# First attention of a four-layer kernel: two more lots of eight projection units with paired 64-row remainders

## The chip, the cores and the metric

The kernel runs on one core of a Trainium2 chip. The metric is the device time of one execution in microseconds, the median of several runs. The engines are named as in the profile: PE (TensorE matmuls), PEld (its weight loads), DVE (VectorE), ACT (ScalarE), POOL (GpSimd) and SP (SyncE, which here issues DMAs only).

## The reference

Four layers with residuals are applied to x of 2048 tokens by 576, in bf16: attention A, mixer B, A, B, and each takes the layer norm of x. Only the attention matters here:

```python
H = 32; Dh = 18; W, dil = 8, 2
q, k, v = split(layernorm(x) @ wqkv)          # 576 -> 3 * 576
logits = q . k[pos - 2 * w], w in 0..7        # * Dh ** -0.5, masked ahead of the start
x = x + (softmax(logits) . v) @ wo
```

The mixer B (4608 wide, with a 2048 x 2048 token matrix) takes most of the time and is not touched.

## The kernel before

The tokens are kept transposed in `xnT` as 128 rows by 5 chunks by 2048 tokens. 576 features are 4 chunks of 128 rows and a remainder of 64 rows, chunk 4. Rows 64 to 127 of chunk 4 come from the last 64 columns of the normalized row (`ln_xn` columns 576 to 639), which are zero in the first attention, and the remainder's weights `wqk4` have zeros in rows 64 to 127, so that chunk 4 is multiplied over whole rows too.

**Projection units.** `PG(d, qk, cc)` computes 128 columns (block d of 5) of q or k (qk) for 512 tokens (cc of 4): five matmuls of 128x512 (L462) into one PSUM bank, a cast of the bank into a staging tile (`evac`, L443 on DVE or L445 on ACT), and, when both halves of 1024 tokens and q and k of a block are staged, DMAs of the staged rows into `QK` ("QK moves"), dealt in turn to the queues of SP and POOL. Block d=4 holds the rest of q and k together. Staging tiles are `stgs` or `lent` parts of `win2a`. A staging tile is written again only when the moves out of it have landed. `PG_run`, which before uses only in the second attention, takes eight units at once in eight banks (three of `X0`, five of the ring): chunks 0 to 3 of the first four, then the eight 64-row remainders alternating between the upper and the lower half of the rows, then chunks 0 to 3 of the other four. For this, the lower half must hold the data and the weights a second time.

**The attention's loop.** The tokens are 17 query tiles, each in two halves of 16 heads: 34 steps s. `L_mm(s)` computes the logits (L536, 16 matmuls; heads are spread over 8 groups g, step 2t needs g 0 to 3 and step 2t+1 g 4 to 7) into a tile of three banks, X, of which there is one, and one of Y. `EXP(s)` is ACT's exponential of the X part and then of the Y part (L545). `PV(s)` multiplies by v (L559) into a ring bank, and DVE normalizes. A step issues L_mm(s+1), EXP(s+1), PV(s) and then what the table `at(s, ...)` lists: projections, `VW(t, hh)` (v of half a tile, L451, cast to `v_ext`), `O_T` (transposes, L595), `WO` (output projection, L629). Because X exists once, L_mm(s+1) waits for the X part of EXP(s). `QK` also has constant rows for the masks, which `fill_window_rows(QK, half)` copies for 1024 tokens from `win_pat` (L201 and L204, DVE).

**The order around the change** is written out by hand for PE, ACT, DVE, POOL and SP; each engine executes its instructions in that order. In the first attention the start is: load x and weights; statistics (`S_`), power for the inverse deviation (`R_`, its power on POOL, L728), normalization (`A_`, L735) and transposes (`T_pe` on PE for tiles 0 to 3, `T_` as DMA transposes issued by SP for the others) for tiles of 128 tokens; `VW` of tiles 0 to 3; `load_pat` on SP; the fill of the first half; 18 units of cc 0 and 1 one after the other, with `R_(12, 4)` behind the units of d=2 of cc 1; eight `VW` (tiles 4 to 7); `A_` and `T_` of tiles 12 to 15; then the list `pre`: four units of cc 2, L_mm(0) and EXP(0), a fifth unit, the fill of the second half, three more units; the two `VW` of tile 8; then the loop. Steps 0 to 9 have one unit each; from step 10 on every step that is not a multiple of four has a `VW`.

Of the kernel before, what the change touches and what calls it, by code (L numbers as in the profile page):

```python
# [18 lines left out]
P = 128  # L19
D = 576  # L20
# [43 lines left out]
class K:  # L64
# [316 lines left out]
    def layer_A(self, li):  # L381
        nc, tc, cfg = self.nc, self.tc, self.cfg
# [9 lines left out]
        QK = main.tile([P, 2, 8, XW], bf16, name="QK")  # L392
# [10 lines left out]
        RING, NSLOT = 6, 2  # L403
        oT = main.tile([P, 5, RING * P], bf16, name="oT")
# [10 lines left out]
        wqk, wqk4, wv_sb, wo_sb = R["wqk"], R["wqk4"], R["wv"], R["wo"]  # L415
# [31 lines left out]
        def VW(t, hh, dve):  # L447
            nk = tdim(t)[0]
            pv = self.PT_tile([P, 512], f32, "pv")
            for c in range(5):  # L450
                nc.tensor.matmul(pv[:nk, 0:288], lhsT=self.xnT[:, c, k0_(t):k0_(t) + nk],  # L451
                                 rhs=wv_sb[:, c, hh * 288:(hh + 1) * 288], start=(c == 0), stop=(c == 4))
            evac(v_ext[:nk, t, 16 * hh:16 * hh + 16, 0:DH], pv[:nk, 0:288].rearrange("p (b d) -> p b d", d=DH), dve)
# [4 lines left out]
        def PG_mm(pp, d, qk, cc, c, start, stop, half=None):  # L458
            w0 = d * P + (640 if qk else 0)
            r0, r1 = (0, P) if half is None else (64 * half, 64 * half + 64)  # L460
            w = wqk[:, c, w0:w0 + P] if c < 4 else wqk4[r0:r1, w0:w0 + P]
            nc.tensor.matmul(pp, lhsT=w, rhs=self.xnT[r0:r1, c, cc * 512:(cc + 1) * 512],  # L462
                             start=start, stop=stop, tile_position=(r0, 0))

        def PG_run(units, queues, on_dve, between=None):
            banks = ([X0[:, k_, :] for k_ in range(3)] +
                     [self.PT_tile([P, 512], f32, "pp")[:, :] for k_ in range(len(units) - 3)])
            n = len(units) // 2
            for u in range(n):
                for c in range(4):  # L470
                    PG_mm(banks[u], *units[u], c, c == 0, False)
            for u in range(2 * n):
                PG_mm(banks[u], *units[u], 4, u >= n, u < n, half=u % 2)
            for u in range(2 * n):
                if u >= n:
                    for c in range(4):
                        PG_mm(banks[u], *units[u], c, False, c == 3)
                if u == n and between:
                    between()
                PG(*units[u], u in on_dve, queues(units[u][0]), pp=banks[u])  # L480

        def PG(d, qk, cc, dve, queues=(nc.sync, nc.gpsimd), pp=None):

            cb, gi = divmod(cc, CBW // 512)
            alone = bool(lent) and d == 4 and cb == 1
            key = (d, cc if alone else cb, alone)
            if key not in stg_tiles:
                if alone:
                    stg_tiles[key] = lent[1]
                elif cb == 0 and d >= 3 and lent:  # L490
                    stg_tiles[key] = lent[d - 3]
                else:
                    stg_tiles[key] = stgs[d if li == 0 else stg_rr[0] % NSTG]
                    stg_rr[0] += 1
                stg_left[key] = 1 if alone else (2 if d < 4 else 1) * (CBW // 512)
            stg = stg_tiles[key]
            if pp is None:
                pp = self.PT_tile([P, 512], f32, "pp")[:, :]
                for c in range(5):
                    PG_mm(pp, d, qk, cc, c, c == 0, c == 4)  # L500
            evac(stg[:, qk, gi * 512:(gi + 1) * 512], pp, dve)
            stg_left[key] -= 1
            if stg_left[key] == 0:
                stg_tiles.pop(key)
                cs = slice(cc * 512, (cc + 1) * 512) if alone else slice(cb * CBW, (cb + 1) * CBW)
                ss = slice(gi * 512, (gi + 1) * 512) if alone else slice(0, CBW)
                moves = []
                for h in range(d * P // DH, H):
                    a, b = max(h * DH, d * P), min((h + 1) * DH, (d + 1) * P)
                    if a >= b:  # L510
                        break
                    g, rg = divmod(h, 4)
                    q0, s0, n = 32 * rg + a - h * DH, a - d * P, b - a
                    if d < 4:
                        moves.append((QK[q0:q0 + n, :, g, cs], stg[s0:s0 + n, :, :]))
                    else:
                        for a_ in range(2):
                            moves.append((QK[q0:q0 + n, a_, g, cs], stg[64 * a_ + s0:64 * a_ + s0 + n, 0, ss]))
                for dst, src in moves:
                    dma_rr[0] += 1  # L520
                    self.dma(dst, src, eng=queues[dma_rr[0] % len(queues)])

        NST = 2 * NT
# [149 lines left out]
        q2 = (nc.gpsimd, nc.sync, nc.gpsimd)  # L673


        if li == 0:
            xts = {}
            spare = oT[:].rearrange("p a b -> p (a b)")[:, 0:4 * D].rearrange("p (i d) -> p i d", d=D)

            def x_load(xg, i0, n, eng):  # L680
                self.dma(xg, self.rows_of(self.A_x, i0, n).rearrange("(i p) d -> p i d", p=P), eng=eng)
# [38 lines left out]
            def S_(*tiles):  # L720
                for i in tiles:
                    B_(i)
                    G_(i)

            def R_(i0, n):
                rs = rstds[:, i0:i0 + n]
                nc.vector.tensor_scalar_add(out=rs, in0=mvs[:, i0:i0 + n, 1], scalar1=EPS)
                nc.gpsimd.tensor_tensor(out=rs, in0=rs, in1=self.neg_half[:, 0:1].to_broadcast([P, n]), op=ALU.pow)  # L728
            xns = {}

            def A_(*tiles):
                for i in tiles:
                    xns[i] = xn = self.xn_bufs[self.xn_rr % len(self.xn_bufs)]
                    self.xn_rr += 1
                    nc.vector.tensor_scalar(out=xn[:, 0:D], in0=xts[i], scalar1=mvs[:, i, 0:1],  # L735
                                            scalar2=rstds[:, i:i + 1], op0=ALU.subtract, op1=ALU.mult)

            def T_pe(i):
                xn = xns.pop(i)
# [7 lines left out]
            def T_(*tiles):  # L747
                for i in tiles:
                    self.ln_T(xns.pop(i), i * P, P)
# [26 lines left out]
            rows[3](nc.gpsimd)  # L776
            A_(6, 7)
            T_(6, 7)
            S_(8)
            self.load_pat(nc.sync)  # L780
            S_(9, 10, 11)
# [3 lines left out]
            T_(8, 9, 10, 11)  # L785
            self.fill_window_rows(QK, 0)
            S_(13, 14, 15)
            order = [(d, cc) for cc in range(2) for d in range(5)]
            for k_, (d, cc) in enumerate(order):
                for qk in ((1, 0) if d < 4 else (0,)):  # L790
                    PG(d, qk, cc, False, (nc.gpsimd, nc.sync) if d in (0, 3, 4) else q2)
                if k_ == 7:
                    R_(12, 4)
            nvw0, nvw = 4, 9
        else:
            def qs(d):
                return (nc.gpsimd, nc.sync) if d == 0 else q2
# [11 lines left out]
            for cc in range(2):  # L809
                PG(4, 0, cc, False, q2)  # L810
            nvw0, nvw = 0, 4
        for t in range(nvw0, nvw - (1 if li == 0 else 0)):
            for hh in range(2):
                VW(t, hh, li == 0 and hh == 0)
        if li == 0:
# [13 lines left out]
        def at(s, f, *a):  # L829
            table.setdefault(s, []).append((f, a))  # L830
        pgs = [(d, qk, cc) for d, cc in ((0, 2), (1, 2), (2, 2), (0, 3), (1, 3), (2, 3), (3, 2), (3, 3), (4, 2), (4, 3))
               for qk in ((1, 0) if d < 4 else (0,))]
        PG_END = 14
        pre, pgs = pgs[:6], pgs[6:]
        if li == 0:
            for u in ((3, 1, 2), (3, 0, 2)):
                pre.append(u)
                pgs.remove(u)
        if li == 0:
            pgs = [u for u in pgs if u[2] == 2] + [u for u in pgs if u[2] > 2]  # L840
        for k_, (d, qk, cc) in enumerate(pgs):
            at(k_ if li == 0 else (k_ * PG_END) // len(pgs), PG, d, qk, cc, True, *((q2,) if li == 0 else ()))
        vws = [(t, hh) for t in range(nvw, NT) for hh in range(2)]
        lag, twice = (PG_END - 5, (PG_END - 2, NST - 2)) if li == 0 else (9, (NST - 2,))
        vsteps = ([x for x in range(PG_END - 4, NST - 3) if x % 4] if li == 0 else
                  [6, 6] + list(range(8, NST)))
        for k_, (t, hh) in enumerate(vws):
            assert vsteps[k_] <= 2 * t - 2 + hh
# [58 lines left out]
            at(s_b + d_b * k_, win2b_piece, k_)  # L907
        at(NST - 2, O_T, NT - 2)
        at(NST, O_T, NT - 1)
        for k_, (d, qk, cc) in enumerate(pre):  # L910
            if k_ == (4 if li == 0 else 0):
                self.ring = ["PT"]
                L_mm(0)
                EXP(0)
            PG(d, qk, cc, li > 0 or k_ < 5, q2)
            if li == 0 and k_ == 4:
                self.fill_window_rows(QK, 1)
        if li == 0:
            VW(nvw - 1, 0, False)
            VW(nvw - 1, 1, False)  # L920
        for s in range(NST):
            if s == NST - 1:
                self.ring = ["PT", "PT", "PT", "Y", "Y"]
# [345 lines left out]
```

## Time and profile before

| | |
|---|---|
| time, median of 3 runs | 1152.67 us (1152.64 to 1152.9) |
| time of the profiled execution | 1152.74 us |
| its span | 1150.9 us |
| granted TensorE clock | 1.00 |
| first projection unit of the first attention | 13.42 us |
| first logits, second, third | 42.16, 48.14, 50.14 us |

All stage times below are microseconds from the span's start. In the views an instruction group has its start and length, the engine, the line, the tiles as out<-in, the shape, the count, and in brackets the idle time in front of it with what ended it. The rows of PE's matmuls overlap: one of 128x512 lasts 0.38 us by its row, and the next starts 0.216 us after it.

### The profile page before, as it was taken

What the parts mean: (1) busy time and instruction counts of PE and PEld (TensorE: products, weight loads), DVE (VectorE), ACT (ScalarE), POOL (GpSimd) and SP (SyncE); (2) the same over time, 40 slices, a digit from 0 to 9 for tenths busy, and PEclk for the clock granted to TensorE, in tenths of its full rate; (3) what the DMA queues carried; (4) which work ended last, traced back from release to release, by engine and by line L of the source; (5) the groups of instructions that cost most, each with busy time, mean ns of one, the idle gap of its engine ahead of it and who ended that gap; (6) DMA issues with size and microseconds to landing.
All of it is one profiled execution on the core that took longest, in us unless ns stands there. A gap on an engine that the chain in (4) does not pass through costs nothing.

```text
span 1150.9 us, 29693 instructions
## 1 busy us (share of the span) xinstructions
PE 1142.6 (99%) x12930; PEld 614.5 (53%) x12949; DVE 539.7 (47%) x1198; ACT 370.5 (32%) x660; POOL 259.6 (23%) x387
## 2 busy tenths in 40 slices
PE   8999999999999999999999999999999999999998
PEld 5567554444444444457755775544444444444676
DVE  8789987312233222244466889843322223222312
ACT  5589565011111111102247876541111111011000
POOL 3689654000000000002153767530000000000000
PEclk9999999999999999999999999999999999999999
DMA  8877696000000000049455867920000000001322
GB/s 195 183 164 200 141 211 137 10 13 13 13 1 13 13 13 2 1 152 213 110 110 110 180 152 176 246 60 1 13 13 13 13 13 1 13 2 30 101 74 58
DMA packets 177372, 91.26 MB, mean 79 GB/s; under 512 B 128788, under 2 KB 170420, under 8 KB 177242
## 3 DMA queue, kind: packets, MB, share of 16 engines
q1 hardware_dynamic: 164762, 70.75, 28.1%
q0 software_dynamic: 5888, 12.72, 4.6%
q10 hardware_dynamic: 6592, 5.90, 1.7%
q8 instruction: 101, 1.65, 0.6%
q14 instruction: 29, 0.24, 0.1%
HBM read 35.46 MB, written 14.69 MB: 44 GB/s over the span
## 4 chain that ended last, share of the span: by engine, by line
PE 97%; ACT 1%; DVE 1%; issue 0%; DVEq 0%; ACTq 0%
PE hh L234 79%; PE pp L462 6%; PE pv L451 3%; PE pw L629 3%; PE O_ps L559 3%; PE L_ps L536 2%; ACT P_sb L545 1%; PE L_ps L462 1%; PE hh L1191 0%; PE pt L595 0%; DVE ln_st L715 0%; DVE ln_xn L735 0%; DVE win_bits L158 0%; ACT v_ext L445 0%; ACT xnT L745 0%
## 5 line engine op out<-in xcount | busy, mean ns | idle before, releaser
L234 PE MATMUL hh<-Wq,Z 64*128 64x512 bf16 x4608 | 505.8, 376 | 0.0
L234 PEld LDWEIGHTS <-Z 64*128 64x128 bf16 x6984 | 339.8, 94 | 310.1
L1095 DVE TENSOR_TENSOR g_tmp<-hh,ln_xn 128x512 f32<-128x512 f32 x144 | 92.8, 686 | 452.3 <-PE hh L234 452.3
L947 ACT COPY bank_turn<-ones 1x1 bf16<-1x1 bf16 x239 | 44.8, 188 | 538.5 <-PE hh L234 538.5
L78 POOL DMA_DIRECT2D wout<-in_B_w_out_dram x4 | 4.3, 1075 | 602.0 <-PE hh L234 602.0
L234 PE MATMUL hh<-wout,Z 64*128 64x288 bf16 x2232 | 137.0, 283 | 0.0
L545 ACT ACTIVATE P_sb<-L_ps 128x1440 bf16<-128x1440 f32 (+3 forms) x136 | 125.0, 971 | 24.6 <-PE L_ps L536 23.2
L234 PE MATMUL hh<-xnT,w 64*128 64x512 bf16 x1152 | 132.2, 376 | 0.0
L234 PE MATMUL hh<-win2a,xnT 64*128 64x512 bf16 (+1 forms) x960 | 118.7, 355 | 0.0
L234 PEld LDWEIGHTS <-xnT 64*128 64x128 bf16 x1440 | 69.9, 94 | 70.0 <-issue 0.5
L1020 DVE BATCH_NORM_STATS2 z_st<-zp 128x6 f32<-128x512 bf16 (+1 forms) x160 | 93.0, 624 | 13.0 <-ACT zp L1018 12.9
L1086 ACT ACTIVATE z1T<-hh 128x1024 bf16<-128x1024 f32 x72 | 73.7, 1024 | 61.9 <-PE hh L234 61.9
L234 PEld LDWEIGHTS <-w 64*128 64x128 bf16 x1152 | 56.1, 94 | 68.3
L1096 DVE TENSOR_TENSOR Z<-g_tmp,z1T 128x512 bf16<-128x512 f32 x144 | 92.4, 683 | 0.0
L1018 ACT ACTIVATE zp<-hh 128x1024 bf16<-128x1024 f32 (+1 forms) x96 | 76.1, 810 | 48.8 <-PE hh L234 48.6
L462 PE MATMUL pp<-xnT,wqk_sb 128*128 128x512 bf16 (+1 forms) x313 | 74.2, 379 | 0.9
L234 PE MATMUL hh<-win2b,xnT 64*128 64x512 bf16 (+1 forms) x480 | 72.8, 355 | 0.0
L1160 DVE TENSOR_TENSOR x_new<-hh,xo 128x288 bf16<-128x288 f32 x64 | 26.3, 453 | 93.0 <-PE hh L234 85.0
L299 POOL TENSOR_SCALAR ln_xn<-x_new,ln_mv,ln_rstd 128x576 bf16<-128x576 bf16 x28 | 64.2, 2293 | 2.7
L78 POOL DMA_DIRECT2D QK<-stg x76 | 48.0, 636 | 36.5 <-DVE stg L443 21.9
L462 PEld LDWEIGHTS <-wqk_sb 128*128 128x128 bf16 (+1 forms) x360 | 32.1, 97 | 36.6 <-issue 1.9
L1044 POOL TENSOR_SCALAR Z<-zp,z_mv,z_rstd 128x256 bf16<-128x256 bf16 x32 | 50.7, 1584 | 3.5
(124 smaller groups left out, 753.3 us busy)
## 6 DMA issues: line engine op xcount, KB each, us to landing
xres<-x_new SPq DMA_DIRECT2D x44, 144.0 KB
wout<-in_B_w_out_dram POOLq DMA_DIRECT2D x4, 1296.0 KB, 7.4
xo<-xres SPq DMA_DIRECT2D x32, 144.0 KB
xn_rows<-ln_xn SPq DMA_DIRECT2D x28, 160.0 KB
w<-in_B_w_in_dram SPq DMA_DIRECT2D x16, 256.0 KB
QK<-stg POOLq DMA_DIRECT2D x51, 72.0 KB, 4.4
QK<-stg SPq DMA_DIRECT2D x37, 72.0 KB
xo<-in_A_x_dram SPq DMA_DIRECT2D x6, 288.0 KB
```

What stands on the lines that cost most here:

```text
L78: return eng.dma_start(out=out, in_=in_)
L234: ins = self.nc.tensor.matmul(outs[a_], lhsT=lhs(a_, c, r0), rhs=rhs(a_, c, r0), start=start and k_ == 0, stop=stop and k_ == len(chunks) ...
L299: e.tensor_scalar(out=xn[:nrows, 0:D], in0=x_t[:nrows, :], scalar1=mv[:nrows, 0:1], scalar2=rstd[:nrows, 0:1], op0=ALU.subtract, op1=ALU.mult)
L462: nc.tensor.matmul(pp, lhsT=w, rhs=self.xnT[r0:r1, c, cc * 512:(cc + 1) * 512], start=start, stop=stop, tile_position=(r0, 0))
L545: nc.scalar.activation(out=P_bufs[2 * jp + s % 2][:nk, :, :, 0:nq], in_=Lv[:nk, :, :, 0:nq], func=ACT.Exp, scale=scale)
L947: self.turn_on = lambda tok: nc.scalar.copy(out=tok, in_=self.ones[0:1, 0:1])
L1018: nc.scalar.activation(out=zp[:, w0:w0 + n], in_=pz, func=ACT.Gelu_apprx_tanh)
L1020: nc.vector.bn_stats(out=st[:, x // 512, :], in_=zp[:, x:x + min(512, w0 + n - x)])
L1044: eng.tensor_scalar(out=Z[:, b0:b1, i, :], in0=zv[:, b0:b1, :], scalar1=mv[:, 0:1], scalar2=rstd[:, 0:1], op0=ALU.subtract, op1=ALU.mult)
L1086: lambda ht, z1T=z1T, q2=q2: nc.scalar.activation(out=z1T[:, q2 * 512:(q2 + 2) * 512], in_=ht[:].rearrange("p a b -> p (a b)"), func=ACT.G ...
L1095: nc.vector.tensor_tensor(out=tmp[:], in0=pg[:, a_, :], in1=bsp[:, qs], op=ALU.add)
L1096: nc.vector.tensor_tensor(out=uT(jj)[:, sub, qs], in0=tmp[:], in1=z1Ts[jj, sub][:, qs], op=ALU.mult)
```

## The change

Eight of the nine units of cc 1 and the eight first units of cc 2 become two calls of `PG_run`. For this the last 64 columns of the normalized rows are copied a second time for tiles 4 to 11 (eight copies on DVE), and the 64 remainder rows of the weights are loaded a second time into rows 64 to 127 of the end of `oT` (two DMAs on SP, ahead of `load_pat`). The second lot is ahead of L_mm(0); the fill of the second half is issued in the middle of this lot, behind its first four casts, of which DVE makes the second and the fourth and ACT the others, as it does the lot's last four. `R_(12, 4)` is issued in the middle of the first lot, behind the moves of d=0 and d=1, where it was behind those of d=2. The unit (4, 0, 2) goes from step 0 to `pre`, its cast from DVE to ACT. The two `VW` of tile 9 go from steps 10 and 11 to step 0, and the later ones are dealt anew, so that steps 10 and 14 have none.

```diff
         def PG_mm(pp, d, qk, cc, c, start, stop, half=None):
...
-            w = wqk[:, c, w0:w0 + P] if c < 4 else wqk4[r0:r1, w0:w0 + P]
+            w4 = wqk4_up if li == 0 and half == 1 else wqk4
+            w = wqk[:, c, w0:w0 + P] if c < 4 else w4[r0:r1, w0:w0 + P]
...
-            spare = oT[:].rearrange("p a b -> p (a b)")[:, 0:4 * D].rearrange("p (i d) -> p i d", d=D)
+            oT_flat = oT[:].rearrange("p a b -> p (a b)")
+            spare = oT_flat[:, 0:4 * D].rearrange("p (i d) -> p i d", d=D)
+            wqk4_up = oT_flat[:, RING * P * 5 - 2 * D:RING * P * 5]
+
+            def load_wqk4_up(eng):
+                for c0, w0 in ((D, D + 64), (0, 0)):
+                    self.dma(wqk4_up[64:128, w0:w0 + 512], self.A_wqkv[512:576, c0:c0 + 512], eng=eng)
...
                     nc.vector.tensor_scalar(out=xn[:, 0:D], in0=xts[i], scalar1=mvs[:, i, 0:1],
                                             scalar2=rstds[:, i:i + 1], op0=ALU.subtract, op1=ALU.mult)
+                    if 4 <= i < 12:
+                        nc.vector.tensor_copy(out=xn[:, D:640], in_=xn[:, 512:D])
...
             T_(6, 7)
+            load_wqk4_up(nc.sync)
             S_(8)
             self.load_pat(nc.sync)
...
-            order = [(d, cc) for cc in range(2) for d in range(5)]
-            for k_, (d, cc) in enumerate(order):
+            for d in range(5):
                 for qk in ((1, 0) if d < 4 else (0,)):
-                    PG(d, qk, cc, False, (nc.gpsimd, nc.sync) if d in (0, 3, 4) else q2)
-                if k_ == 7:
-                    R_(12, 4)
-            nvw0, nvw = 4, 9
+                    PG(d, qk, 0, False, (nc.gpsimd, nc.sync) if d in (0, 3, 4) else q2)
+            PG_run([(d, qk, 1) for d in range(4) for qk in (1, 0)],
+                   lambda d: (nc.gpsimd, nc.sync) if d in (0, 3) else q2, (), lambda: R_(12, 4))
+            PG(4, 0, 1, False, (nc.gpsimd, nc.sync))
+            nvw0, nvw = 4, 10
...
-        for t in range(nvw0, nvw - (1 if li == 0 else 0)):
+        for t in range(nvw0, 8 if li == 0 else nvw):
...
-            for u in ((3, 1, 2), (3, 0, 2)):
+            for u in ((3, 1, 2), (3, 0, 2), (4, 0, 2)):
...
-            at(k_ if li == 0 else (k_ * PG_END) // len(pgs), PG, d, qk, cc, True, *((q2,) if li == 0 else ()))
+            at(k_ + 1 if li == 0 else (k_ * PG_END) // len(pgs), PG, d, qk, cc, True, *((q2,) if li == 0 else ()))
...
-        vsteps = ([x for x in range(PG_END - 4, NST - 3) if x % 4] if li == 0 else
+        vsteps = ([x for x in range(PG_END - 3, NST - 3) if x % 4 and x != PG_END] if li == 0 else
...
+        if li == 0:
+            PG_run(pre[:8], lambda d: q2, (1, 3), lambda: self.fill_window_rows(QK, 1))
+            pre = pre[8:]
         for k_, (d, qk, cc) in enumerate(pre):
-            if k_ == (4 if li == 0 else 0):
+            if k_ == 0:
                 self.ring = ["PT"]
                 L_mm(0)
                 EXP(0)
-            PG(d, qk, cc, li > 0 or k_ < 5, q2)
-            if li == 0 and k_ == 4:
-                self.fill_window_rows(QK, 1)
+            PG(d, qk, cc, li > 0, q2)
         if li == 0:
-            VW(nvw - 1, 0, False)
-            VW(nvw - 1, 1, False)
+            VW(8, 0, False)
+            VW(8, 1, False)
+            at(0, VW, 9, 0, True)
+            at(0, VW, 9, 1, False)
```

## The prediction

> **What bounds the kernel now.** The page first:
>
> ```profile
> PE 1142.6 (99%) x12930; PEld 614.5 (53%) x12949; DVE 539.7 (47%) x1198; ACT 370.5 (32%) x660; POOL 259.6 (23%) x387
> ...
> PE 97%; ACT 1%; DVE 1%; issue 0%; DVEq 0%; ACTq 0%
> ```
>
> PE is busy for 99% of the span and is 97% of the chain that ended last. So whatever PE is spared comes off the time, and whatever PE is made to wait goes onto it. The change lies between 13 and 82 us, so next come PE's instructions in order of time there (start, length, line, tiles, count).
>
> ```profile
> 13.42 19.59 PE L462 MATMUL pp<-xnT,wqk_sb 128*128 128x512 bf16 x88
> 32.84 5.06 PE L451 MATMUL pv<-wv_sb,xnT 128*128 128x288 bf16 x40
> 37.74 4.48 PE L462 MATMUL pp<-xnT,wqk_sb 128*128 128x512 bf16 x19
> 42.16 0.40 PE L536 MATMUL L_ps<-QK 32*128 32x128 bf16 x16
> ...
> 48.14 0.40 PE L536 MATMUL L_ps<-QK 32*128 32x128 bf16 x16
> ...
> 50.14 0.39 PE L536 MATMUL L_ps<-QK 32*128 32x120 bf16 x16 [0.23 <-ACT P_sb L545]
> ```
>
> The 18 units of the first 1024 tokens are 90 matmuls (two records are missing) in 32.84 - 13.42 = 19.42 us: 0.216 us a matmul, 1.08 us a unit, without a pause. Eight VW follow in 37.74 - 32.84 = 4.90 us. The first logits, L_mm(0), come at 42.16, L_mm(1) at 48.14, L_mm(2) at 50.14 after a wait of 0.23 us. Before has next to nothing to win in waits here, and much to lose.
>
> **The pairs.** In a lot, eight 64-row remainders run two at a time: 36 slots for 40. Before runs the same routine in its second attention:
>
> ```profile
> 580.65 2.76 PE L462 MATMUL L_ps<-xnT,wqk_sb 128*128 128x512 bf16 x11
> ...
> 584.22 0.60 PE L462 MATMUL L_ps<-xnT,wqk_sb 64*128 64x512 bf16 x3
> ...
> 588.65 1.03 PE L462 MATMUL L_ps<-xnT,wqk_sb 128*128 128x512 bf16 x4
> ...
> 584.86 1.56 ACT L445 CAST stg<-L_ps 128x512 bf16<-128x512 f32 x3 [1.94 <-PE pp L462]
> ```
>
> The first and third row are the starts of its first and second lot: 8.00 us for one. (The others, its first remainder and its first cast, are used below.) 40 slots are 8.64 us, so a lot saves 0.64 us and two save 1.28 us. Pure pairing would be 36 x 0.216 = 7.78 us a lot; 0.22 us more is paid for going from whole rows to half rows and back. The Trainium skill, "TensorEngine Tiling (Array Packing)", Tiling Modes, states that changing the tiling mode drains TensorE; the trace agrees with 0.22 us for two changes. By its "up to 2x" for 64 rows the two lots would save 1.73 us instead.
>
> **The copies on DVE.** A_ gets eight copies of 128x64, each waiting for the operation in front of it. The nearest row is the fill's own:
>
> ```profile
> 24.71 2.36 DVE L201 COPY QK<-win_pat 128x4096 bf16<-128x4096 bf16 x2 [0.39 <-DMA win_pat<-win_period]
> 27.11 0.18 DVE L204 COPY QK<-win_pat 128x64 bf16<-128x64 bf16 x1
> 27.20 2.35 DVE L201 COPY QK<-win_pat 128x4096 bf16<-128x4096 bf16 x2
> ...
> 44.45 4.62 DVE L201 COPY QK<-win_pat 128x4096 bf16<-128x4096 bf16 x4
> ```
>
> From 24.71 + 2.36 = 27.07 to 27.20 is 0.13 us. Two big copies take 2.36 us and four 4.62 us, so neighbours that don't wait for each other overlap by 0.10 us, which is lost too. One copy costs about 0.20 us (bounds 0.13 and 0.25), eight 1.6 us. The fill of the first half then starts later by 1.6 less the 0.39 us for which it waited anyway: 1.2 us. The transposes of tiles 4 to 7 land about 0.5 us later, which I put at nothing: cc=1 starts at 23.1, and their issue ends at 20.2 before.
>
> **SP.** The two loads of load_wqk4_up come between these transposes and load_pat:
>
> ```profile
> 4.59 4.50 SPq L78 DMA_DIRECT2D wqk_sb<-in_A_wqkv_dram  x6
> ...
> 14.03 6.20 SPq L306 DMA_TRANSPOSE xnT<-ln_xn  x4
> 21.81 1.60 SPq L78 DMA_DIRECT2D win_pat<-win_period  x4
> ```
>
> At 4.50 / 6 = 0.75 us each they fill the gap from 20.23 to 21.81; load_pat starts some 0.4 us later, which the late fill covers (if not, the fill waits as it does now). Their data are wanted at 26.7, when the first lot reaches its remainders. SP's own QK moves then begin about 0.8 us later, behind tiles 8 to 11.
>
> **POOL's queue of QK moves** decides the rest. POOL issues 23 moves for the first 1024 tokens:
>
> ```profile
> 28.02 6.28 POOL L78 DMA_DIRECT2D QK<-stg  x9 [5.19 <-DVE QK L204]
> ...
> 37.78 1.04 POOL L728 TENSOR_TENSOR lnx_rstd<-lnx_rstd,neg_half 128x4 f32<-128x4 f32 x1
> 38.77 4.84 POOL L78 DMA_DIRECT2D QK<-win2a  x8
> ```
>
> It is released by the fill and then never pauses to 43.61: nine moves, six more (d=2), R_(12,4)'s power, eight of d=3 and d=4. In the change the start is 1.2 us later and the power goes ahead of the six, so that d=2 comes 2.2 us later and d=4, the last four, from 41.2 + 1.2 = 42.4 on. Before, the fill of the second half began at 44.45, behind the last issue. In the change it stands right behind the two casts that DVE has in the second lot. PE is there at 23.13 + 8.00 + 1.08 + 4.90 = 37.1, the first banks are done 4.2 us later (584.86 - 580.65 there), and the casts take 1.3 us: the fill runs from about 42.5 to 47.1, on top of d=4. What that does, the second attention shows:
>
> ```profile
> 597.44 4.62 DVE L201 COPY QK<-win_pat 128x4096 bf16<-128x4096 bf16 x4
> ...
> 596.55 5.62 POOL L78 DMA_DIRECT2D QK<-stg  x5
> ...
> 602.17 2.90 POOL L78 DMA_DIRECT2D QK<-stg  x5
> ...
> 597.59 4.87 SPq L78 DMA_DIRECT2D QK<-stg  x6
> ```
>
> Five moves on POOL take 5.62 us while DVE copies and 2.90 us after it: about one passes for each copy of 1.15 us. SP's take 0.81 us all the same. The Trainium skill, "DMA: Bandwidth & Descriptors", SWDGE vs HWDGE vs iDMA, states that GpSimd writes its descriptors to SBUF, that DVE locks it out of there during 2-port modes, and that DMAs from SP are immune; by that rule the change is in trouble here, and the trace agrees (5.62 against 2.90 us). So the last issue runs from about 46.2 to 47.3 instead of 44.3 to 44.8. From issue to landing:
>
> ```profile
> QK<-win2a POOLq DMA_DIRECT2D x1, 36.0 KB, 4.6
> ...
> DMA to landing us min/median/max: 4.3/4.3/4.3
> ...
> DMA to landing us min/median/max: 3.5/4.9/7.5
> ```
>
> 4.6 us is the last move before (43.1 to 47.7, just 0.4 us ahead of L_mm(1)), 4.3 us one under the second attention's copies, and the third row is all QK moves from 26 to 52 us. I take 4.7, between the like case's 4.3 and the 5.2 that the last move of before becomes with 0.6 us more of issue: d=4 has landed at 50.9 (bounds by the third row, 49.7 and 53.7).
>
> **Who waits for d=4.** The last four matmuls of L_mm(1), which need the last heads, and the cast of (4,0,2), which overwrites lent[1], from which d=4 is moved. Before, that cast was DVE's and came at step 0; now it is ACT's and stands ahead of two v_ext casts and EXP(1).
>
> ```profile
> 42.69 1.94 ACT L545 ACTIVATE P_sb<-L_ps 128x1536 bf16<-128x1536 f32 x2 [4.34 <-PE L_ps L536]
> 44.91 0.59 ACT L445 CAST stg<-pp 128x512 bf16<-128x512 f32 x1 [0.28 <-ACT P_sb L545]
> ...
> 48.24 0.40 ACT L445 CAST v_ext<-pv 128x288 bf16<-128x288 f32 x1 [0.21 <-PE pv L451]
> 48.64 3.82 ACT L545 ACTIVATE P_sb<-L_ps 128x1536 bf16<-128x1536 f32 x4
> ```
>
> From 50.9, 0.59 + 0.40 + 0.40 us, a little overlapped (1.3), puts EXP(1) at 52.2 against 48.64, and L_mm(2), which waits for its X part, 3.6 us later too: 53.7. PE cannot use the time: PV(0) needs the bank of (4,0,2), the two moved VW are done by 53.5, and PE's own work would have reached L_mm(2) at 50.14 - 1.28 + 1.26 = 50.1. EXP(0) is late too, but not on the path: d=2's last move, issued 0.58 us ahead of the power's 37.78 before, is issued near 39.4 and, at the median 4.9 us, landed at 44.3; four casts (2.2 us) and EXP(0) (1.94 us) end at 48.5, two microseconds ahead of 50.9. The loop after L_mm(2) is the same in both, and PE-bound to step 9, so the lateness is kept.
>
> **What comes back.** Steps 10 and 14 lose a VW each. From the chain in order of time:
>
> ```profile
> 69.24 0.32 PE L_ps L536 x16
> ...
> 71.68 0.32 PE L_ps L536 x16
> ...
> 78.24 0.32 PE L_ps L536 x16
> ...
> 80.30 0.32 PE L_ps L536 x16
> ...
> 82.35 0.38 PE L_ps L536 x16
> ...
> 84.20 0.39 PE L_ps L536 x16
> ```
>
> A step with little PE work is 1.85 us (82.35 to 84.20: logits, their exponentials, the next logits), so step 14 can fall from 2.06 to 1.85 and step 10 from 2.44 to about 1.95: 0.7 us (bounds 0.2, if ACT is behind, and 1.26, all of both VW).
>
> **The sum.** +3.6 - 0.7 = +2.9 us; the 1.28 us of the pairs are inside the 3.6, since PE waits anyway. The profiled execution took 1152.74 us (span 1150.9), 0.07 us over the median of 1152.67. So 1152.7 + 2.9 = **1155.6 us**.
>
> **Rivals.**
> - *The fill and d=4 miss each other* (the copies cost less, or the casts hold the fill back). Then d=4 lands at 47.7 + 1.2 = 48.9, EXP(1) starts at 50.2, L_mm(2) is 1.6 us late, less 0.7: +0.9, 1153.6 us. Against it: one move of shift either way still leaves three under the copies. For it: all of this is a matter of 0.6 us per move. Chance 0.18.
> - *The moves are in time, and the gain stays* (the eight copies vanish in DVE's waits). This decides if d=4 has landed by about 47.9. Then EXP(0) runs at 45.8 behind the last cast of the lot, EXP(1) at 48.5, L_mm(2) at 50.0, and steps 10 and 14 give 0.7: -0.8, 1151.9 us. To be faster by over 2.3 us all of the 1.28 and 1.26 us would have to come off at once. For it: the pairs are sure. Against it: the fill has only 0.39 us of slack and the moves 0.4 us. Chance 0.12.
> - *The last moves get caught in what SP issues next* (tiles 12 to 15, then xo and wo_sb). With 7.0 us instead of 4.7, d=4 lands at 53.2: +5.2, 1157.9 us. The 7.5 us in the row above was such a case. Chance 0.08.
> - That the pairs would not overlap is excluded by the 8.00 us lot.
>
> **The numbers.** The forecast has 0.62. Its own range, from 49.7 us and 52.4 us for d=4's landing, is 1154.4 to 1157.1. With the first rival inside and the other two left out, the range is 1152.4 to 1157.6. A change under 0.2% (2.3 us) is about what a measurement of this kernel can tell from none. Slower by more, over 1155.0: most of the forecast, 0.48 (d=4 landed after 50.3), and the third rival, 0.08: 0.56. Within: the rest of the forecast, the first rival and most of the second: 0.41. Faster: 0.03.
>
> **What would show it.** Right: lots of 8.0 us at 23 and 37 us; the fill of the first half at about 25.9; four POOL moves of over 1 us near 43 to 47; EXP(1) near 52.2 and L_mm(2) near 53.7, with the ACT cast of (4,0,2) released by a DMA; the same steps as before to step 9. Wrong: POOL done before the second fill, or EXP(1) before 50.

## The result, and the profile after

| | before | after |
|---|---|---|
| time, median of 6 runs | 1152.79 us (1152.53 to 1153.44) | 1157.48 us (1156.79 to 1158.61) |
| ratio | | 1.0036 (95%: 1.0026 to 1.0046) |
| profiled execution, its span | 1152.74, 1150.9 us | 1158.61, 1156.8 us |
| L_mm(0), L_mm(1), L_mm(2) | 42.16, 48.14, 50.14 | 45.16, 50.19, 56.09 |
| first matmul of the mixer (L234) | 121.40 | 126.67 |

The change makes the kernel slower by 4.7 us by the medians, 0.4%. The profiled execution of after is the longest of its six runs, so what it shows is the upper end, and those of e3, e4 and e11 below are among the shortest of theirs. From L_mm(2) on it is 5.95 us late, from the mixer on 5.27 us.

The page of after, its busy times and its chain:

```profile
PE 1144.9 (99%) x12949; PEld 615.8 (53%) x12949; DVE 538.4 (47%) x1202; ACT 371.6 (32%) x664; POOL 261.9 (23%) x387
...
PE 95%; ACT 1%; POOL 1%; DMA 1%; DVE 1%; issue 1%; DVEq 0%; ACTq 0%
```

POOL and DMA have come into the chain, which before had 97% PE and neither of them. Where, PE in order of time says:

```profile
23.12 2.75 PE L463 MATMUL L_ps<-xnT,wqk_sb 128*128 128x512 bf16 x12
...
37.09 2.75 PE L463 MATMUL L_ps<-xnT,wqk_sb 128*128 128x512 bf16 x12
...
45.16 0.40 PE L537 MATMUL L_ps<-QK 32*128 32x128 bf16 x16
47.36 1.24 PE L463 MATMUL pp<-xnT,wqk_sb 128*128 128x512 bf16 x5 [1.80 <-ACT stg L445]
...
50.19 0.60 PE L537 MATMUL L_ps<-QK 32*128 32x128 bf16 x14 [0.36 <-ACT P_sb L546]
51.56 0.22 PE L537 MATMUL L_ps<-QK 32*128 32x128 bf16 x1 [0.78 <-DMA QK<-win2a]
52.20 0.23 PE L537 MATMUL L_ps<-QK 32*128 32x128 bf16 x1 [0.41 <-DMA QK<-win2a]
53.17 0.58 PE L560 MATMUL O_ps<-v_ext,P_sb 128*128 128x19 bf16 x16 [0.75 <-ACT win2a L445]
53.60 2.56 PE L451 MATMUL pv<-wv_sb,xnT 128*128 128x288 bf16 x10
56.09 0.45 PE L537 MATMUL L_ps<-QK 32*128 32x120 bf16 x16
```

The lots run at 23.12 and 37.09. The last matmuls of L_mm(1) wait for moves out of `win2a`, which is d=4, until 52.20, PV(0) for the cast of (4,0,2) until 53.17, and then the two VW of tile 9 take 2.56 us instead of the 1.39 us of the same ten matmuls at tile 8. POOL's queue in the same time:

```profile
29.32 6.25 POOL L78 DMA_DIRECT2D QK<-stg  x9 [5.65 <-ACT stg L445]
35.59 1.03 POOL L735 TENSOR_TENSOR lnx_rstd<-lnx_rstd,neg_half 128x4 f32<-128x4 f32 x1
36.58 3.74 POOL L78 DMA_DIRECT2D QK<-stg  x6
40.32 1.84 POOL L78 DMA_DIRECT2D QK<-win2a  x3
42.98 5.38 POOL L78 DMA_DIRECT2D QK<-win2a  x5 [0.82 <-DMA QK<-stg]
```

It starts at 29.32, waits 0.82 us for the landing of an earlier move, and needs 5.38 us for the last five moves. DVE has the two fills, and ACT goes on when d=2 and d=4 have landed:

```profile
25.99 2.36 DVE L201 COPY QK<-win_pat 128x4096 bf16<-128x4096 bf16 x2
28.39 0.18 DVE L204 COPY QK<-win_pat 128x64 bf16<-128x64 bf16 x1
...
43.14 4.62 DVE L201 COPY QK<-win_pat 128x4096 bf16<-128x4096 bf16 x4
```

```profile
27.31 1.56 ACT L445 CAST stg<-L_ps 128x512 bf16<-128x512 f32 x3 [3.40 <-PE pp L463]
...
46.73 1.07 ACT L445 CAST stg<-pp 128x512 bf16<-128x512 f32 x2 [3.48 <-DMA QK<-stg]
...
48.64 1.99 ACT L546 ACTIVATE P_sb<-L_ps 128x1536 bf16<-128x1536 f32 x2
52.53 0.58 ACT L445 CAST win2a<-pp 128x512 bf16<-128x512 f32 x1 [1.91 <-PE L_ps L537]
53.02 0.71 ACT L445 CAST v_ext<-pv 128x288 bf16<-128x288 f32 x2
53.60 1.97 ACT L546 ACTIVATE P_sb<-L_ps 128x1536 bf16<-128x1536 f32 x2
```

POOL's row names a cast as what released the first move, but it is the fill that held it. The first move begins 28.39 + 0.18 = 28.57 to 29.32, 0.75 us, behind the fill's first small copy (L204), as before the change, where it was 27.29 to 28.02, 0.73 us. In all profiles but those of e2 and e4 it begins 3.31 to 3.35 us after the fill does. The lot's first casts alone would have let it go at about 28.7, as e4 shows below. The casts at 46.73, ahead of EXP(0), wait for d=2. The chain that ended last, in order of time, goes from the landing of a move out of `stg` (37.17 to 42.70) over POOL's last moves, the landing of the last one (47.86 to 52.15), the last matmul of L_mm(1), the cast of (4,0,2), PV(0) and the two VW of tile 9 to L_mm(2).

Last, the windows (start:end, length, busy time and instructions of PE, PEld, DVE, ACT and POOL, then the granted clock, the DMA share and GB/s):

```profile
50.70:53.20 2.50, 0.56 (x5) 0.31 (x5) 0.00 (x0) 0.67 (x2) 0.00 (x0) 0.93 1.18 277
53.20:56.10 2.90, 2.90 (x30) 1.72 (x29) 1.17 (x3) 2.37 (x4) 2.69 (x6) 0.50 1.11 354
56.10:60.00 3.90, 3.90 (x78) 2.33 (x78) 2.12 (x5) 3.68 (x5) 0.91 (x2) 0.98 0.38 102
```

PE was busy for 0.56 of the 2.50 us in the first row. In finer windows the granted clock falls to 0.50 at 52.85 and is back at 1.00 at 56.26.

### The profile page after: what moved, and what is told of

Same layout as the page of the kernel before. It is cut to its first block, busy times and chain, and to the rows that moved or that the text cites. A ratio compares the mean times of both kernels' runs of the same rounds, so it can differ in the third digit from the quotient of the medians.

```text
span 1156.8 us, 29718 instructions
## 1 busy us (share of the span) xinstructions
PE 1144.9 (99%) x12949; PEld 615.8 (53%) x12949; DVE 538.4 (47%) x1202; ACT 371.6 (32%) x664; POOL 261.9 (23%) x387
## 4 chain that ended last, share of the span: by engine, by line
PE 95%; ACT 1%; POOL 1%; DMA 1%; DVE 1%; issue 1%; DVEq 0%; ACTq 0%
PE hh L234 79%; PE pp L463 4%; PE pv L451 3%; PE pw L630 3%; PE O_ps L560 2%; PE L_ps L537 2%; ACT P_sb L546 1%; POOL QK L78 1%; PE L_ps L463 1%; DMA QK<-stg 0%; PE hh L1204 0%; DMA QK<-win2a 0%; DVE ln_st L722 0%; PE pt L596 0%; ACT stg L445 0%
## 5 line engine op out<-in xcount | busy, mean ns | idle before, releaser
L234 PE MATMUL hh<-Wq,Z 64*128 64x512 bf16 x4608 | 505.8, 376 | 0.0
L234 PEld LDWEIGHTS <-Z 64*128 64x128 bf16 x6984 | 340.3, 94 | 309.6
L234 PE MATMUL hh<-wout,Z 64*128 64x288 bf16 x2232 | 137.0, 283 | 0.0
L234 PE MATMUL hh<-xnT,w 64*128 64x512 bf16 x1152 | 132.2, 376 | 0.0
L234 PE MATMUL hh<-win2a,xnT 64*128 64x512 bf16 (+1 forms) x960 | 118.7, 355 | 0.0
L234 PEld LDWEIGHTS <-xnT 64*128 64x128 bf16 x1440 | 70.0, 94 | 69.9 <-issue 0.5
L234 PEld LDWEIGHTS <-w 64*128 64x128 bf16 x1152 | 56.1, 94 | 68.2
L234 PE MATMUL hh<-win2b,xnT 64*128 64x512 bf16 (+1 forms) x480 | 72.8, 355 | 0.0
L463 PE MATMUL pp<-xnT,wqk_sb 128*128 128x512 bf16 (+1 forms) x294 | 68.2, 379 | 1.8 <-ACT stg L445 1.8
L1057 POOL TENSOR_SCALAR Z<-zp,z_mv,z_rstd 128x256 bf16<-128x256 bf16 x32 | 50.8, 1588 | 3.5
```

Source lines behind the costliest of these rows:

```text
L234: ins = self.nc.tensor.matmul(outs[a_], lhsT=lhs(a_, c, r0), rhs=rhs(a_, c, r0), start=start and k_ == 0, stop=stop and k_ == len(chunks) ...
L1057: eng.tensor_scalar(out=Z[:, b0:b1, i, :], in0=zv[:, b0:b1, :], scalar1=mv[:, 0:1], scalar2=rstd[:, 0:1], op0=ALU.subtract, op1=ALU.mult)
```

## The experiments

All ratios are to the kernel before on the same chip (its medians there: 1152.96, 1152.95 and 1152.86 us). The times of stages are those of one profiled execution each; the medians are of 4 to 11 runs.

| | POOL's moves from | EXP(1) | L_mm(2) | median us | ratio, 95% |
|---|---|---|---|---|---|
| before | 28.02 | 48.64 | 50.14 | 1152.79 | |
| after | 29.32 | 53.60 | 56.09 | 1157.48 | 1.0036 (1.0026 to 1.0046) |
| e1 fill in steps 0 to 3 | 29.38 | 52.67 | 55.15 | 1158.76 | 1.0048 (1.0034 to 1.0061) |
| e2 copies on ACT | 37.21 | 58.76 | 60.30 | 1163.25 | 1.0089 (1.0075 to 1.0102) |
| e3 second lot only | 29.23 | 50.45 | 51.98 | 1155.82 | 1.0024 (1.0015 to 1.0034) |
| e4 first lot only | 28.63 | 48.63 | 50.55 | 1154.03 | 1.0009 (1.0000 to 1.0018) |
| e5 PE kept busy | 29.39 | 51.93 | 53.46 | 1156.06 | 1.0032 (1.0019 to 1.0045) |
| e6 lots unpaired | 29.37 | 53.64 | 56.13 | 1158.79 | 1.0048 (1.0036 to 1.0061) |
| e7 copies on POOL | 29.35 | 52.86 | 55.11 | 1158.08 | 1.0041 (1.0028 to 1.0054) |
| e8 last moves by ACT | 29.18 | 50.54 | 52.07 | 1160.30 | 1.0060 (1.0046 to 1.0073) |
| e9 first lot of six | 28.40 | 48.72 | 50.59 | 1152.90 | 1.0000 (0.9991 to 1.0009) |
| e10 both lots mended | 28.47 | 50.86 | 52.43 | 1154.46 | 1.0010 (1.0001 to 1.0019) |
| e11 one cast on DVE | 29.30 | 51.20 | 53.05 | 1156.71 | 1.0034 (1.0021 to 1.0047) |

**e1_fill_in_steps.** Is it the fill on top of d=4?

```diff
-            PG_run(pre[:8], lambda d: q2, (1, 3), lambda: self.fill_window_rows(QK, 1))
+            PG_run(pre[:8], lambda d: q2, (1, 3), None)
+            for k_ in range(4):
+                at(k_, self.fill_piece, QK, k_)     # one of the four copies
```

> The changed kernel, with the fill of the second half taken out of the second lot: its four copies are issued one at a time in steps 0 to 3. Theory (the fill slows POOL's last QK moves, and these hold the cast of (4,0,2) and EXP(1)): POOL's last five moves pass in 0.55 us each instead of 1.15, they are issued by 45.7 instead of 48.4 and have landed by about 49.5 instead of 52.15; EXP(1) is then held by ACT's own queue, behind EXP(0), and starts near 51.8, L_mm(2) near 53.4 instead of 56.1, and the clock is not halved. DVE pays for the copies in steps 0 to 3: 0 to 2 us. Time 1154.8 to 1156.8 us. Rival (the DMA rings are so far behind that the time of issue doesn't matter): d=4 lands at 51 to 52 all the same, L_mm(2) stays at 55 to 56, and with DVE's copies on top the time is 1157.5 us or more.

The late pieces overwrite rows of the third 512 tokens that have been moved already: this part of q and k is changed in e1. POOL's last moves in e1:

```profile
43.20 0.57 POOL L78 DMA_DIRECT2D QK<-win2a  x1 [0.90 <-DMA QK<-stg]
44.12 1.12 POOL L78 DMA_DIRECT2D QK<-win2a  x2 [0.35 <-issue]
45.95 0.52 POOL L78 DMA_DIRECT2D QK<-win2a  x1 [0.71 <-DMA QK<-stg]
46.70 0.51 POOL L78 DMA_DIRECT2D QK<-win2a  x1 [0.22 <-DMA QK<-stg]
```

Without the fill the five moves take 2.72 us instead of 5.38. But now the queue waits for earlier moves to land, 0.90, 0.71 and 0.22 us, and ends at 47.2 where 48.4 had been: of 2.7 us, 1.2 us come back there and 0.9 us at EXP(1). The expected 53.4 for L_mm(2) was far off, and the clock was halved here too. It is the rival's numbers that came: the last matmul of L_mm(1) could begin at 51.27, L_mm(2) at 55.15, and the time is 1158.76 us. The pieces also stand in DVE's way in later steps. So the fill does slow these moves, but it is one of two limits next to each other: without it the landings hold the queue nearly as long.

**e2_copies_on_act.** The eight copies by ACT instead of DVE (`nc.scalar.copy` for `nc.vector.tensor_copy`).

> The changed kernel, with the eight 128x64 copies on ACT instead of DVE. By the prediction's step (the copies delay the fill, the fill releases POOL), the fill starts near 24.7 instead of 26.0, POOL's moves 1.2 us earlier, near 28.1, L_mm(2) 1.2 us earlier, near 54.9, and the time is near 1156.3 us. Rival: POOL is released by the cast of the first lot's second unit (28.9 us), which is as late without the copies; POOL then starts at 29.3 as now, wins at most 0.5 to 1 us because the fill no longer lies on its first move, and the time is 1156.5 to 1157.5 us.

It failed for a reason of its own, which PE and ACT show:

```profile
25.01 6.80 PE L463 MATMUL pp<-xnT,wqk_sb 128*128 128x512 bf16 x20 [6.16 <-ACT stg L445]
```

```profile
23.21 1.26 ACT L745 COPY ln_xn<-ln_xn 128x64 bf16<-128x64 bf16 x4 [5.25 <-DVE ln_xn L742]
```

The copies of tiles 8 to 11 stand ahead of the casts of cc 0 in ACT's order and wait for DVE until 23.21; PE runs out of banks for 6.16 us. It says nothing of the copies' price.

**e3_second_lot_only and e4_first_lot_only.** One lot, with the copies, `pre`, steps and VW that belong to it, the other 512 tokens as before.

> The first lot is undone (the units of cc=1 one after the other, R_(12, 4) behind d=2, copies for tiles 8 to 11 only); all else is as in the changed kernel. Theory: POOL's moves run as before the change and are issued by 43.6 us, the second fill comes at about 43.8, behind them, and d=4 lands near 47.7: EXP(0) near 46.3, EXP(1) near 49.4, L_mm(2) near 50.9 (50.1 before the change), steps 10 and 14 give 0.7 us back: 1152.4 to 1153.2 us, the same as before the change. Rival (the order of the second lot, with the casts ahead of EXP(0), is the loss): L_mm(2) 2 us late or more, 1154.5 us or more.

> Only the first lot, with R_(12, 4) in its middle and copies for tiles 4 to 7; from the VW of tile 4 on the order is that before the change. Theory: POOL starts 1.3 us late (released by the lot's late casts), d=2 is another 1 us late, d=4 lands near 49.3; L_mm(0) and EXP(0) are early as before, L_mm(1) waits for d=4 and EXP(1) starts near 49.5 instead of 48.6: 0.8 to 1.2 us over before, 1153.6 to 1154.0 us, and PE wins nothing from the pairs. Rival (the late moves of the first lot are the whole loss): 1156 us or more. Rival (the first lot alone keeps its 0.64 us): 1152.2 us.

e4 took the expected time. For e3 the same time as before was expected, and its median is 2.86 us over it: the rival's "1154.5 us or more" came. Each lot costs time by itself, the second more than the first. At L_mm(2) the profiles show a loss of 0.41 us with the first lot, 1.84 us with the second and 5.95 us with both, which looks like more than a sum. But these are single executions, and e3's took 1154.29 us, 1.5 us under its median, where after's is 1.1 us over its own. By the medians it is 1.07 and 2.86 us, 3.93 together, against 4.69 us, with intervals of about 1 us either way: that the two lots cost more than their sum is not shown.

e3 started POOL later than expected, at 29.23 and not 28.0. Of this 0.75 us were there before the copies: POOL's first power began at 16.99, in before at 16.24. The four copies of tiles 8 to 11, right ahead of the fill, add the rest. e4 shows what POOL does when the fill is early (the copies of tiles 4 to 7 alone cost it little) and the lot's casts are as late as in after (27.25 for 27.31):

```profile
25.09 2.36 DVE L201 COPY QK<-win_pat 128x4096 bf16<-128x4096 bf16 x2
```

```profile
28.63 6.05 POOL L78 DMA_DIRECT2D QK<-stg  x9 [5.01 <-ACT stg L445]
```

Here the first move begins 3.54 us after the fill, at the cast of the lot's second unit. Further on in e4 it is the last matmuls of L_mm(1) that wait for moves, and PE is bound from there on:

```profile
48.37 0.23 PE L537 MATMUL L_ps<-QK 32*128 32x128 bf16 x1 [0.34 <-DMA QK<-win2a]
48.80 0.23 PE L537 MATMUL L_ps<-QK 32*128 32x128 bf16 x1 [0.21 <-DMA QK<-win2a]
```

**e5_busy_tensor_engine.**

```diff
                 g = 4 * hf + ftl
+                if li == 0 and s == 1 and ftl == 3:
+                    for _ in range(32):
+                        nc.tensor.matmul(L_tiles[s][0][:, 0, ftl * P:ftl * P + P], lhsT=self.ident[:], rhs=self.ident[:], ...)
```

> 32 idle-purpose matmuls (identity by identity, 128 columns, about 0.056 us each, 1.8 us together, overwritten by the logits that follow) stand in L_mm(1) ahead of its last four matmuls, where TensorE only waits for the last moves. Theory (the halved clock after that wait costs 1.0 us on the path): the clock stays at 1.0, the two VW of tile 9 take 1.4 us instead of 2.56, L_mm(2) starts at 55.0 to 55.2 instead of 56.09, about 1.0 us less in all: 1156.5. Rival (the clock costs nothing, the path is ACT's and the moves'): L_mm(2) stays at 56.1, time 1157.5.

```profile
49.60 1.96 PE L538 MATMUL L_ps<-ident 128*128 128x128 bf16 x32
51.49 0.23 PE L541 MATMUL L_ps<-QK 32*128 32x128 bf16 x4
51.66 0.56 PE L564 MATMUL O_ps<-v_ext,P_sb 128*128 128x19 bf16 x16
52.08 1.39 PE L451 MATMUL pv<-wv_sb,xnT 128*128 128x288 bf16 x10
53.46 0.39 PE L541 MATMUL L_ps<-QK 32*128 32x120 bf16 x16
```

The VW take 1.39 us and L_mm(2) follows EXP(1) by 53.46 - 51.93 = 1.53 us, like before (1.50), where after has 56.09 - 53.60 = 2.49: the halved clock costs 0.96 us there. The other 1.67 us by which L_mm(2) is earlier are not the edit's: EXP(1) itself came at 51.93, because POOL's last moves were issued by 47.0 in this execution and not by 48.4:

```profile
44.93 2.02 POOL L78 DMA_DIRECT2D QK<-win2a  x2 [0.24 <-DMA QK<-stg]
```

The median is 1.4 us below after's, 1.0 us of it expected, and the intervals of the two ratios overlap.

**e6_unpaired_lots.** `half=u % 2 if li > 0 else None`.

> The two lots of the first attention with their remainders as full 128-row matmuls one by one; all else as in the changed kernel. Lots of 8.64 us, L_mm(0) at about 46.4 instead of 45.16. Theory (the 1.28 us of the pairs lie inside TensorE's waiting for the moves): L_mm(2) at 55.8 to 56.5, time 1157.5 within 0.6. Rival (the pairs' gain is on the path, and something else lost the more): L_mm(2) at 57.4, time 1158.8.

L_mm(0) came at 46.51, as 8.64 us a lot make it, and L_mm(2) at 56.13 against 56.09: at that point the 1.28 us of the pairs are worth nothing. The mixer starts at 126.87 here and at 126.67 in after. The two profiled executions, 1158.79 and 1158.61 us, differ as little. But 1158.79 is also the median of e6, at the rival's number and 1.31 us over after's, and the two intervals overlap. So the profiles say that the pairs are not on the path, and the times leave it open.

**e7_copies_on_pool.** `nc.gpsimd.tensor_copy` for the eight copies.

> The eight 128x64 copies issued by POOL, which has next to nothing before the first moves, instead of DVE. The fill of the first half goes back from 25.99 to about 24.8. Theory (the moves' start is held by two things, the fill and the cast of the lot's second unit at 28.9): POOL starts at 28.9 instead of 29.32, L_mm(2) 0.4 us earlier at about 55.7, time about 1157.1. Rival (the copies alone are the late start): POOL starts at 28.1, L_mm(2) at 54.9, time 1156.2.

```profile
26.03 2.36 DVE L201 COPY QK<-win_pat 128x4096 bf16<-128x4096 bf16 x2 [1.65 <-DMA win_pat<-win_period]
```

```profile
29.35 2.82 POOL L78 DMA_DIRECT2D QK<-stg  x3 [4.61 <-ACT stg L445]
```

Both theories missed, since the fill stayed at 26.03, now held by `win_pat`: SP's transposes of tiles 4 to 7 end at 21.51 instead of 20.59, and the two loads of the weights stand ahead of `load_pat`. POOL's first move stayed with the fill, 3.32 us behind it. The copies are one of three things that are late together; the others are `win_pat` and, up to about 28.7, the lot's casts.

**e8_last_moves_by_act.** POOL's four moves of d=4 are collected and issued by ACT behind the VW of tiles 4 to 7.

> The four moves of d=4 that POOL issued last are issued by ACT, behind the VW of tiles 4 to 7 (ACT is idle there from 37.7 to 41.3). Theory (POOL's queue decides when d=4 has landed): they have landed by about 46, POOL ends with d=3 near 44.5 and that lands near 48.5, L_mm(1) waits for no move; EXP(1) then stands behind EXP(0) (50.6) and three casts, at 51.9 instead of 53.6, L_mm(2) at 53.4 to 53.6, no halved clock: time about 1154.9. Rival (the transfers themselves are full, whoever issues them): L_mm(1) still waits for moves until 51 or 52, L_mm(2) at 55 to 56, time 1156.5 to 1157.5.

```profile
52.07 0.39 PE L542 MATMUL L_ps<-QK 32*128 32x120 bf16 x16 [0.17 <-ACT P_sb L551]
...
57.21 0.61 PE L464 MATMUL pp<-xnT,wqk_sb 128*128 128x512 bf16 x1 [4.25 <-DMA xnT<-ln_xn]
```

```profile
40.00 7.92 SPq L78 DMA_DIRECT2D QK<-win2a  x8
48.02 6.36 SPq L306 DMA_TRANSPOSE xnT<-ln_xn  x4
```

L_mm(2) came at 52.07, 4.0 us earlier than in after and earlier than expected, with the clock full until then: POOL's queue of moves is the path up to L_mm(2). But SP's eight moves started at 40.00 instead of 37.50, behind two waits for landings, so the transposes of tiles 12 to 15 went out at 48.02 instead of 44.01, and PE waited 4.25 us for them. L_mm(1) still waited 0.37 us for a move, at 49.34, which was not expected. In PE's long wait the clock fell to 0.50, from about 55.2 to 62. The time is the second worst of all. Moving the issue to another queue moved the lateness to another user of the same transfers.

**e11_cast_on_dve.** `PG(d, qk, cc, True, q2)` for (4,0,2).

> The changed kernel with one edit: the cast of (4,0,2) on DVE, so that ACT has the two v_ext casts behind it done while the moves are still under way. Theory (the three casts stacked on ACT ahead of EXP(1) cost what they take, 1.1 to 1.3 us): EXP(1) at 52.5 instead of 53.60, L_mm(2) at 54.6 if the clock is full and 55.5 if it is halved, time 1156.3 within 0.7. Rival (EXP(1) waits for the moves, not for ACT): EXP(1) at 53.4 or later, time 1157.5.

```profile
50.94 0.45 PE L537 MATMUL L_ps<-QK 32*128 32x128 bf16 x2 [0.45 <-DMA QK<-win2a]
...
53.05 0.39 PE L537 MATMUL L_ps<-QK 32*128 32x120 bf16 x16
```

```profile
51.20 1.94 ACT L546 ACTIVATE P_sb<-L_ps 128x1536 bf16<-128x1536 f32 x2 [0.32 <-PE L_ps L537]
```

The second of the two matmuls in the first row began at 51.16. EXP(1) starts 0.04 us later, in after 53.60 - 52.20 = 1.40 us after the last matmul of L_mm(1) began: the stack on ACT costs 1.4 us. Here, too, the moves were ready earlier than in after, by 1.0 us, although nothing ahead of them differs. In e11 the first of POOL's last five moves went out at 42.68, ahead of the fill, and in after at 42.98, just as the fill began, so that the last one began at 46.75 here and at 47.86 there. So a small shift ahead of the fill moves d=4 by a microsecond from one execution to the next, and how much of the 0.77 us between the two medians is the cast's stays open.

**e9_first_lot_of_six and e10_both_lots_mended.** The loads of the upper weights on POOL, d=0's units singly ahead of a lot of six, the power behind d=2's moves; e9 with the first lot alone, e10 with both, the copies of tiles 8 to 11 on POOL, L_mm(0) and EXP(0) ahead of the second lot's last four casts, and e11's cast.

```diff
-            load_wqk4_up(nc.sync)
+            load_wqk4_up(nc.gpsimd)                  # behind rows[3]
...
-            PG_run([(d, qk, 1) for d in range(4) for qk in (1, 0)], ..., (), lambda: R_(12, 4))
+            for qk in (1, 0):
+                PG(0, qk, 1, False, (nc.gpsimd, nc.sync))
+            PG_run([(d, qk, 1) for d in range(1, 4) for qk in (1, 0)], ..., (), lambda: R_(12, 4), at_u=4)
...
-            PG_run(pre[:8], lambda d: q2, (1, 3), lambda: self.fill_window_rows(QK, 1))
+            PG_run(pre[:8], lambda d: q2, (1, 3), lambda: self.fill_window_rows(QK, 1), mid=first_logits)  # e10
```

> First lot alone, and of six units only (d=1 to 3): the two units of d=0 are done singly ahead of it, the two loads of the upper weight copy go to POOL near 19 us instead of SP, and R_(12,4)'s power stands behind d=2's moves, as before. Theory (what the first lot loses is the late start of POOL's moves, held by the lot's late first casts and the late fill): fill at 24.8 and POOL's start at 28.1 instead of 28.63, L_mm(0) at 41.7, the last matmuls of L_mm(1) no later than 48.1, L_mm(2) at 49.8 to 50.1: time 1152.4 to 1153.0, against 1154.03 with the lot of eight. Rival (the lot costs for another reason): L_mm(2) at 50.5, 1154.0.

> Both lots with every cause taken away that the runs have named: first lot of six behind d=0's two units, loads of the upper weight copy on POOL, copies of tiles 8 to 11 on POOL, R_(12,4)'s power behind d=2's moves, L_mm(0) and EXP(0) ahead of the last four casts of the second lot, the cast of (4,0,2) on DVE. Theory: POOL starts at 28.1 to 28.5 instead of 29.32, L_mm(0) at 43 to 44 instead of 45.16, d=4 landed by 49, L_mm(2) at 50.8 to 51.5 instead of 56.09, no halved clock; steps 10 and 14 give 0.7 back: time 1152.8 to 1153.8. Rival (two lots fill the transfers so that the moves are late anyway): L_mm(2) at 54 or more, time over 1155.5.

POOL in e10, and PE:

```profile
28.47 9.74 POOL L78 DMA_DIRECT2D QK<-stg  x15 [2.03 <-DVE QK L204]
38.23 1.05 POOL L740 TENSOR_TENSOR lnx_rstd<-lnx_rstd,neg_half 128x4 f32<-128x4 f32 x1
39.23 4.57 POOL L78 DMA_DIRECT2D QK<-win2a  x8
```

```profile
47.96 1.24 PE L463 MATMUL pp<-xnT,wqk_sb 128*128 128x512 bf16 x5 [1.23 <-ACT stg L445]
...
50.36 0.40 PE L542 MATMUL L_ps<-QK 32*128 32x128 bf16 x16
```

e10's POOL queue is that of before, 0.45 us later and without a pause, done at 43.8 ahead of the fill (44.20), and L_mm(1) waits for no move. 3.0 of the 4.7 us are gone by the medians. What is left are other waits: the lot has taken all eight banks, EXP(0) stands ahead of its last casts, and PE waits 1.23 us for one of these banks. PE also stands for 0.76 us at 23.97, until the cast of the unit just before is done, which it does not in e9; this puts L_mm(0) at 44.50. L_mm(2) at 52.43 missed the expected 50.8 to 51.5, and the time of 1154.46 us missed the expected 1152.8 to 1153.8. e9 is as fast as before and no faster. It has the expected time, but not by the expected way: its L_mm(1) still waits for moves, to 48.85, and L_mm(2) is at the rival's place, no earlier than in e4 (50.59 and 50.55), so that e9's gain on e4, 1.1 us by the medians, isn't in this place and stays unexplained. Its lot of six has L_mm(0) at 41.73, 0.43 us ahead of before, and nothing of this is left at L_mm(2). By the medians no version beat before.

## Why the prediction was right

The time was forecast at 1155.6 us with a range up to 1157.6, slower by over 0.2% at 0.56. It is 1157.48. The path is the one forecast, but not the size: of the 4.7 us by the medians 2.9 were forecast. The forecast's own range ended at 1157.1. The time lies in the wide one by 0.12 us only, and no row of the prediction is worked out to that upper end, so that it holds is in part luck.

- **The lots**: right. 8.0 us each; L_mm(0) at 45.16, worked out as 45.1. That their gain lies inside PE's waiting is what the profile of e6 shows at L_mm(2); its median doesn't confirm it.
- **The copies**: right. The fill came at 25.99 for 25.9, and POOL behind it 1.30 us late for 1.2. Left out were two things that are nearly as late: the lot's first banks, done 4.2 us after its start, whose casts let POOL go at 28.63 in e4, and `win_pat`, which in e7 holds the fill by itself.
- **The last moves under the fill**: right in what the fill does, four moves at 1.14 to 1.48 us, but too much was put on it: without the fill (e1) EXP(1) is only 0.93 us earlier. That POOL would otherwise run without a pause was wrong: it waits for landings of earlier moves (0.82 us in after, 1.8 us in e1). Why these hold it is not shown. This is the step that was missing, and d=4 is ready at 52.20, by L_mm(1), for 50.9, inside the bounds of 49.7 to 53.7. Profiles of kernels that are alike up to there had it 1.0 us earlier (e11), so part of this miss is scatter.
- **ACT's stack**: right. 1.4 us from the last wait to EXP(1), for 1.3, and in e11 it is gone. The sign that a DMA releases the cast of (4,0,2) is not there in after, whose row names L_mm(1)'s last matmul; in e5 and e8 a DMA out of `win2a` does release it, at 50.87 and 49.48, before that matmul is done.
- **EXP(0) off the path**: right, though the casts ahead of it, which wait for d=2, began at 46.73 where d=2 was forecast to land at 44.3, and it ended at 50.6 and not 48.5, 1.9 us ahead of the cast that decided.
- **Steps 10 and 14**: right. 0.68 us of the 5.95 us come back by the mixer's start, for 0.7.
- **The halved clock**: missed altogether. It adds 0.96 us in after, by the comparison with e5.

For the profiled execution the sum of L_mm(2) is then: the last issue ended at 48.36 and not 43.61, +4.75 (1.30 the late start; 2.38 the eight last moves, 1.84 + 5.38 for 4.84; 0.82 the wait for a landing; 0.25 the other fifteen); from its start to the landing 4.3 us for 4.6, -0.3; from there to EXP(1) 1.40 us for 0.94, +0.5; the clock +1.0. That is 5.95. Forecast were 3.6.

Of the rivals, the moves caught in what SP issues next (1157.9 us) gave nearly the measured time, by another way: d=4's last two moves on POOL landed 4.8 and 4.3 us after their issue began and not 7. It was d=2's last move that landed late, 6.7 us after its issue. The other two are excluded by four slow moves and by EXP(1) at 53.60. Not explained are 0.6 us between the mixer's start and the end, by which the profiled executions of several of these kernels differ.

## What to carry to other kernels

In these profiles a stage that waits for transfers hides a faster TensorE altogether: look first for the transfers' queue, what starts it and what stands in it, and only then for the matmuls. Computing in lots finishes the same work earlier but its first results later, and holds all the banks; whoever feeds a queue with these first results pays for it. And stage times that come from one execution each can't be added up: by them the two lots cost 0.4, 1.8 and together 6.0 us, by the medians 1.1, 2.9 and together 4.7.

## What the hardware showed unexpectedly

PE's wait had a price behind it. The granted clock was 0.50 from 52.85 to 56.26, and ten matmuls took 2.56 instead of 1.39 us; the same in e6 and e1, and 2.34 us in e7. In e11, with the last moves ready 1.0 us earlier, and in e5, with 32 matmuls in it, it stayed at 1.00. The Trainium skill, "TensorE: Matmul & The Clock Gate", Part 1 (The HAM clock gate), states that the clock halves after an idle window of about 3.4 us; the trace agrees in the kind, but here no gap was as long: in the 3.4 us ahead of the fall, from 49.45 to 52.85, PE was busy for 1.43 us.

The transfers pushed back: POOL and SP did not merely take 0.6 and 0.8 us a move, by the profile they stood still until earlier moves had landed, POOL for 0.82 us in after, and SP in e8, where ACT issued too, for 0.8 and 1.9 us, so that its last eight moves began 2.5 us later. Whether the kernel's own order or the queue makes them wait is not shown.
